# Sliding-window attention and a two-layer tanh-shrink block: another order of the early loads and of the steps of three batches

## The chip, the cores and the metric

The kernel runs on one core of one Trainium2 chip. The metric is the device time of one execution in microseconds. The core has five engines that run side by side and wait for each other through semaphores: TensorE (PE: matrix products; its weight loads are listed apart as PEld), VectorE (DVE), ScalarE (ACT), GpSimd (POOL) and SyncE (SP, which here only issues transfers). Transfers run on 16 DMA engines. ACT and SP issue through hardware queues, GpSimd through a software queue[...].

## The reference, cut to what matters

```python
# q, k, v: [8 batches, 8 heads, 576 positions, 64], float32
scores = scale * np.matmul(q, k.transpose(0, 1, 3, 2))
rel = pos[:, None] - pos[None, :]
mask = (rel >= 0) & (rel < 64)                 # causal window of 64 keys
attn = softmax(np.where(mask, scores, -1e9))
attn_out = np.matmul(attn, v)
x = attn_out.transpose(0, 2, 1, 3).reshape(4608, 512)   # tokens x (heads * dim)
h = x @ w_in                                   # 512 -> 2048, the first layer
g = h - np.tanh(h)
out = g @ w_out                                # 2048 -> 512, the second layer
```

## The kernel before

Two heads make a pair; a batch has four pairs, so pair `g` is pair `g % 4` of batch `g // 4`. A batch has nine blocks of 64 queries; each sees the 64 keys of its own block and the 64 before. The tokens go through the two layers in nine chunks of 512; a chunk has 16 first-layer tiles (`hp_mm`, line L259, then `tanh`, L262, then `g_sub`, L268) and 16 second-layer steps (`yp_mm`, L278). The loop counts half steps `h`: a first-layer tile on each even one, a second-layer step of the chunk before on each odd one from 33 on, and whatever attention work a plan sets beside them:

```python
for h in range(min(items), 2 * (16 * NC + LAG) + 2):      # LAG = 16
    ...
    if h % 2 == 0:
        ...
        if 0 <= c < NC:
            hidden = hp_mm(c, m)
    elif 0 <= cy < NC:
        yp_mm(cy, sy)
    for fn in items.get(h, []):          # the plan's steps
        fn[0](*fn[1:])
    if h % 2 == 0 and 0 <= c < NC:
        g_sub(c, m, *hidden)
```

The first-layer tiles take turns in two PSUM banks (`m % 2`); so tile `m` has to wait for the subtraction of tile `m - 2`.

Batches 0 to 2 (pairs 0 to 11) are placed by a script, `PLAN`; key -1 is what is done ahead of the loop. Each word is a step: a letter, numbers (base 36) and the engines that do it (`p` GpSimd, `a` ACT, `v` DVE, `s` SP). The batches after these follow a fixed pattern that the change leaves alone.

```python
if what in "qr":   load(*n, ...)         # one pair of q, or (r) of k
elif what in "QK": load_all(...)         # a whole batch of q or k, by GpSimd
elif what == "V":  load_v_all(*n)        # a whole batch of v, by GpSimd
elif what == "a":  cast(*n, "q", *eng)   # q of a pair to bf16 rows
elif what == "b":  cast(*n, "k", *eng)
elif what == "v":  load_v(*n)            # one pair of v, by GpSimd
elif what == "d":  cast_v(*n, *eng)      # v of a pair into vb
elif what == "k":  keys_v(*n, *eng)      # "key move": block j, vb -> vw
elif what == "z":  shift_v(...)          # all blocks, upper half of vw -> lower half of the next
elif what == "E":  tr(*n, "q", 3, *eng)  # transposes of q, and two moves to qT
elif what == "F":  tr(*n, "k", ...)      # transposes of k, and a move to kT
elif what == "R":  scores(*n, (4, 0, 1)[n[1]] if n[0] < NP else 4)   # 3 blocks, then exp
elif what == "P":  pv of 9 blocks; norm(*n)
elif what == "X":  x_tr(...)             # transposes of the attention output to xT
# w, o: loads of w_in, w_out; M: masking; i, n, m: constants
```

The parts that V goes through (`vb` and the two `vw` are single buffers, `vb` for all batches, `vw` for even and odd ones):

```python
vw = [const.tile([128, NJ, H, D + 1], BF16, name=f"vw{i}") for i in range(2)]
vb = const.tile([PV, EV, H, D + 1], BF16, name="vb")

def load(g, n, eng):                     # one pair
    if eng is nc.gpsimd:                 # bf16, cast by the transfer, in a part of the batch's tile
        ...
    else:                                # float32, in a tile of its own
        t = qk_pool.tile([P, 2, E * D], F32, tag=n + "f", name=n + "f")
    eng.dma_start(out=t, in_=...)

def keys_v(b, j, eng=nc.sync):           # 64 keys of all heads, 65 KB
    eng.dma_start(out=vw[b % 2][64:128, j]..., in_=vb[8 * j:8 * j + 8]...)

def shift_v(b, j0, j1, eng=nc.sync):
    lo, hi = vw[b % 2][0:64, j0 + 1:j1 + 1], vw[b % 2][64:128, j0:j1]
    if eng is nc.vector:
        eng.tensor_copy(lo, hi)          # on DVE, in two parts
    else:
        eng.dma_start(out=lo..., in_=hi...)

def norm(g):                             # DVE: a reciprocal and two products
    ...
```

Of the kernel before, what the change touches and what calls it, by code (L numbers as in the profile page):

```python
# [15 lines left out]
def kernel(  # L16
# [289 lines left out]
    def play(script):  # L306
        for step in script.split():
# [48 lines left out]

    PLAN = {
        -1: """
            q0a v03 i a0v v00 v02 r0a r1a b0a E0va F0v v01 q1a d02v m q2a d01p R01 r2a q3s
            d00a d03v R02 k00s k07p k01p k02s a1a k03a b1v F1a k04a k05p k08s k06a E1av r3s a2p R12 z0v  # L360
            R00 E2vv R10 K1 n V1 P0 b2a b3p Q1 a3v F2a w0 R11 P1 R22 F3a R21 R20 E3va
            R31 P2 b5p d13a R30 w1 R32 d12v P3 a4p d10a d11a a5a a7p w2 X011v k18s k13s X000v b4p
            k16a k15s k14a k17a X001v X010a b6p k10s k11s k12a Q2 a6p K2 V2 z1s b7p o0 o1 a8p a9p
            o3 b8p d20p F4v d21p d22p d23p E4aa b9p k25s o2 k23p k27s k22s bAp""",
        5: "k26s F5a R41",
        10: "R40 bBp aAp E5av R42 k20s k24s R50 k21s P4",
        11: "R52 E6aa R51 P5 E7vv F6a",
        15: "F7v R60 X100v R62",
        16: "R61 k28s",
        19: "R70 P6 R72 F8a R71 E8av",  # L370
        22: "R80",
        23: "z2s P7",
        24: "E9av",
        26: "X110a aBp X101v",
        27: "R82 F9a R81 X111a",
        30: "FAv M8",
        31: "R92 R91",
        35: "R90 M9",
        41: "P9 FBa EAav",
        43: "P8 RA0 EBaa RA1",  # L380
        45: "RA2 MA",
        50: "X200v PA RB0",
        51: "X201v",
        52: "RB1 RB2",
        53: "MB",
        56: "PB",
        60: "X210v",
        62: "X211a",
    }
# [31 lines left out]
    for h in range(min(items), 2 * (16 * NC + LAG) + 2):  # L421
        n = h // 2
        c, m = divmod(n, M)
# [41 lines left out]
```

The softmax here doesn't subtract the row's maximum and nothing guards it: scores larger than these inputs give would overflow.

## Time and profile before

| | before |
|---|---|
| time, median of 3 | 375.83 us (375.75 to 377.02) |
| span of the profiled execution | 374.0 us |
| busy: PE, DVE, ACT, POOL | 327.9, 213.7, 193.9, 99.6 us |
| first first-layer tile (L259) starts | 44.94 us |
| first second-layer step (L278) in the chain of waits | 90.08 us |
| PE busy from 0 to 75 us, from 75 to 374 us | 39.75 us, 288.19 us |
| moved by DMA | 37.88 MB, mean 101 GB/s |

The profile's page divides the span in 40 slices with the busy share in tenths; the views of the trace (windows, chain of waits, list of waits, timeline) give the same execution in more detail. In all of them `vw<-vb` is a key move, `vw<-vw` the shift, `vall` a load of V, and `ps` the PSUM tile into which every matrix product goes.

### The profile page before, as it was taken

What the parts mean: (1) busy time and instruction counts of PE and PEld (TensorE: products, weight loads), DVE (VectorE), ACT (ScalarE), POOL (GpSimd) and SP (SyncE); (2) the same over time, 40 slices, a digit from 0 to 9 for tenths busy, and PEclk for the clock granted to TensorE, in tenths of its full rate; (3) what the DMA queues carried; (4) which work ended last, traced back from release to release, by engine and by line L of the source; (5) the groups of instructions that cost most, each with busy time, mean ns of one, the idle gap of its engine ahead of it and who ended that gap; (6) DMA issues with size and microseconds to landing.
All of it is one profiled execution on the core that took longest, in us unless ns stands there. A gap on an engine that the chain in (4) does not pass through costs nothing.

```text
span 374.0 us, 6004 instructions
## 1 busy us (share of the span) xinstructions
PE 327.9 (88%) x2289; PEld 192.4 (51%) x2329; DVE 213.7 (57%) x354; ACT 193.9 (52%) x352; POOL 99.6 (27%) x133
## 2 busy tenths in 40 slices
PE   2236565888898999999999999999999999999996
PEld 2226434555554655555555555555555554444442
DVE  2326623686666767777666767676766643443400
ACT  4324454476575665556556556656565344444321
POOL 5606331824417503630543064121000000000000
PEclk9999677699999999999999999999999999999999
DMA  8799998574965855935594458044000001001012
GB/s 180 163 157 152 204 203 160 85 139 78 184 119 96 153 100 129 142 75 106 119 155 80 94 111 142 28 94 112 32 29 30 28 30 56 30 28 56 30 56 84
DMA packets 31980, 37.88 MB, mean 101 GB/s; under 512 B 3536, under 2 KB 25808, under 8 KB 31504
## 3 DMA queue, kind: packets, MB, share of 16 engines
q0 software_dynamic: 19648, 17.45, 31.5%
q1 hardware_dynamic: 10552, 17.82, 16.9%
q10 hardware_dynamic: 1752, 2.24, 2.2%
q8 instruction: 18, 0.29, 0.3%
q14 instruction: 10, 0.08, 0.1%
HBM read 36.70 MB, written 9.44 MB: 123 GB/s over the span
## 4 chain that ended last, share of the span: by engine, by line
PE 78%; DMA 11%; ACT 4%; DVE 3%; issue 2%; ACTq 0%; POOL 0%; DVEq 0%; SPq 0%; POOLq 0%
PE ps L278 33%; PE ps L259 31%; DMA vw<-vb 7%; PE ps L224 4%; PE ps L210 4%; PE ps L197 4%; DMA vw<-vw 2%; PE ps L241 2%; DMA vall<-in_v_dram 2%; DVE xs L235 1%; DVE qt L81 1%; ACT pt L214 1%; ACT th L262 1%; ACT vb L79 1%; ACT kt L79 1%
## 5 line engine op out<-in xcount | busy, mean ns | idle before, releaser
L259 PE MATMUL ps<-xT,wi 128*128 128x512 bf16 x553 | 147.7, 386 | 4.7 <-DVE gT L268 3.1
L268 DVE TENSOR_TENSOR gT<-ps,th 128x512 bf16<-128x512 f32 x144 | 99.2, 690 | 81.4 <-ACT th L262 80.3
L278 PE MATMUL ps<-w_out_sb,gT 128*128 128x512 bf16 x559 | 143.0, 379 | 1.1 <-ACT ysb L283 0.2
L262 ACT ACTIVATE th<-ps 128x512 f32<-128x512 f32 x144 | 86.1, 598 | 83.8 <-PE ps L259 80.0
L259 PEld LDWEIGHTS <-wi 128*128 128x128 bf16 x576 | 61.7, 115 | 50.3 <-issue 7.9
L278 PEld LDWEIGHTS <-gT 128*128 128x128 bf16 x576 | 53.6, 98 | 51.3 <-issue 0.5
L214 ACT ACTIVATE pt<-ps 128x384 bf16<-128x384 f32 x96 | 46.8, 490 | 51.3 <-PE ps L210 37.7
L235 DVE TENSOR_TENSOR xs<-ps,rc 64x576 bf16<-64x576 f32 x64 | 48.3, 755 | 1.5
L210 PE MATMUL ps<-qt,kt 128*128 128x128 bf16 x288 | 37.2, 229 | 10.5 <-DVE qt L81 4.6
L81 POOL COPY vb<-vall 72x1024 bf16<-72x1024 bf16 x25 | 26.2, 1057 | 68.5 <-DMA vw<-vb 45.2
L224 PE MATMUL ps<-vw,pt 128*128 128x130 bf16 x288 | 30.4, 231 | 12.2 <-DVE vw L133 6.2
L224 PEld LDWEIGHTS <-pt 128*128 128x128 bf16 x288 | 23.0, 103 | 25.4 <-issue 8.6
L81 POOL COPY qb<-qall 96x768 bf16<-96x768 bf16 x27 | 22.3, 827 | 48.8 <-PE ps L197 29.1
L81 DVE COPY qt<-ps 64x576 bf16<-64x576 bf16 x31 | 23.5, 758 | 16.8 <-ACT qt L79 15.3
L210 PEld LDWEIGHTS <-kt 128*128 128x128 bf16 x288 | 24.9, 104 | 11.5 <-issue 2.3
L81 POOL COPY kb<-kall 96x768 bf16<-96x768 bf16 x28 | 23.2, 830 | 25.4 <-PE ps L197 9.6
L283 ACT ACTIVATE ysb<-ps 128x512 f32<-128x512 f32 x36 | 21.4, 594 | 15.1 <-PE ps L278 15.1
L79 ACT ACTIVATE qt<-ps 64x576 bf16<-64x576 bf16 x33 | 21.0, 636 | 7.1 <-DMA vw<-vb 3.4
L79 ACT ACTIVATE kt<-ps 128x576 bf16<-128x576 bf16 x28 | 18.1, 646 | 11.7 <-PE ps L197 11.6
L81 DVE COPY xT<-ps 128x512 bf16<-128x512 bf16 (+4 forms) x40 | 13.5, 364 | 16.8 <-PE ps L241 16.8
L197 PE MATMUL ps<-ident,qb 96*128 96x96 bf16 x192 | 15.0, 219 | 5.6 <-DVE qb L81 4.8
L197 PE MATMUL ps<-ident,kb 96*128 96x96 bf16 x192 | 15.2, 221 | 5.1 <-DVE kb L81 3.8
(48 smaller groups left out, 150.4 us busy)
## 6 DMA issues: line engine op xcount, KB each, us to landing
out_dram<-ysb SPq DMA_DIRECT2D x36, 256.0 KB
kall<-in_k_dram POOLq DMA_DIRECT2D x7, 576.0 KB, 9.3
vall<-in_v_dram POOLq DMA_DIRECT2D x7, 576.0 KB, 10.3
qall<-in_q_dram POOLq DMA_DIRECT2D x7, 576.0 KB, 6.2
vw<-vb SPq DMA_DIRECT2D x61, 65.0 KB
vw<-vw SPq DMA_DIRECT2D x7, 520.0 KB
w_out_sb<-in_moe_w_out_dram POOLq DMA_DIRECT2D x4, 512.0 KB, 12.0
wi<-in_moe_w_in_dram POOLq DMA_DIRECT2D x2, 512.0 KB, 9.2
```

Of the source, the lines that this page charges most:

```text
L79: nc.scalar.activation(o, i, ACT.Copy)
L81: eng.tensor_copy(o, i)
L197: nc.tensor.transpose(tp[:, e, :], src[:, e, :], ident[:P, :P])
L210: nc.tensor.matmul(sp[:, i, :], kT[g % NR][:, 64 * j:64 * j + 128], qT[g % NR][:, :, 64 * j:64 * j + 64], start=True, stop=g >= 2 * NP)
L214: nc.scalar.activation(PT[g % NPT][:, 3 * grp:3 * grp + 3, :], sp, ACT.Exp, scale=scale)
L224: nc.tensor.matmul(ps[:, 5 + grp, 130 * i:130 * i + 130], PT[g % NPT][:, j, :], vw[b % 2][:, j, 2 * pr:2 * pr + 2, :], start=True, stop=True)
L235: nc.vector.tensor_tensor(xo[r, :, :, pr, :], ov[r, :, :, h, 0:D], rc[r].to_broadcast([64, 3, 3, 64]), ALU.mult)
L259: nc.tensor.matmul(hp, w_in_tile(ki, m), chunk_tile(c)[:, ki, :], start=(ki == 0), stop=(ki == 3))
L262: nc.scalar.activation(th, hp, ACT.Tanh)
L268: nc.vector.tensor_tensor(gT[c][:, m, :], hp, th, ALU.subtract)
L278: nc.tensor.matmul(yp, gT[c][:, m, s * 128:(s + 1) * 128], w_out_sb[:, m, :], start=(m == 0), stop=(m == M - 1))
L283: nc.scalar.activation(ysb, ps[:, yp_bank(c, s), :], ACT.Copy)
```

## The change

It alters the script only. Among the early loads, four single pairs (k of pairs 1 and 2, q of pairs 2 and 3) now go through GpSimd with the cast on the way, and four (q0, k0, q1, k3) stay in the hardware queues; the loads of V come ahead of most of them. GpSimd does one key move of batch 0 and then issues the whole-batch loads V1 and K1. All nine key moves of batch 1 are issued by SP, and their shift (`z1v`) is done by DVE and no longer by a transfer (`z1s`). Pairs 4 to 11 are set at other half steps: pair 4's value product, `P4`, goes from 10 to 12, pair 5's from 11 to 15, and so on. Its purpose is to let the early loads and key moves of batch 0 through first, to take V of batch 1 off the path, and to spread the attention of three batches over the first-layer tiles in another way.

```diff
     PLAN = {
         -1: """
-            q0a v03 i a0v v00 v02 r0a r1a b0a E0va F0v v01 q1a d02v m q2a d01p R01 r2a q3s
-            d00a d03v R02 k00s k07p k01p k02s a1a k03a b1v F1a k04a k05p k08s k06a E1av r3s a2p R12 z0v
-            R00 E2vv R10 K1 n V1 P0 b2a b3p Q1 a3v F2a w0 R11 P1 R22 F3a R21 R20 E3va
-            R31 P2 b5p d13a R30 w1 R32 d12v P3 a4p d10a d11a a5a a7p w2 X011v k18s k13s X000v b4p
-            k16a k15s k14a k17a X001v X010a b6p k10s k11s k12a Q2 a6p K2 V2 z1s b7p o0 o1 a8p a9p
-            o3 b8p d20p F4v d21p d22p d23p E4aa b9p k25s o2 k23p k27s k22s bAp""",
-        5: "k26s F5a R41",
-        10: "R40 bBp aAp E5av R42 k20s k24s R50 k21s P4",
-        11: "R52 E6aa R51 P5 E7vv F6a",
-        15: "F7v R60 X100v R62",
-        16: "R61 k28s",
-        19: "R70 P6 R72 F8a R71 E8av",
...
+            q0a i v00 a0v v02 v03 v01 d00v d02a r0s b0a r1p q1a E0vv r2p m d03p F0a d01v q3p
+            R01 b2a k05s b1a a1v k00s k08a k01p k02a R02 k04a k06s F1a E1vv q2p V1 a2v R00 R12 K1
+            a3p n k07s F2a Q1 k03s z0v w0 d13p w1 K2 E2aa R11 P0 r3s R10 b3a b5p E3va P1
+            R21 b6p w2 b4p Q2 d10p F3v a4p R20 d11p R22 P2 V2 d12a k17s k12s k16s k10s R30 k18s
+            b7p o3 R32 R31 X001v a7p o2 P3 X010v o0 a5p X000v X011a E4vv a9p b8p""",
+        0: "F4a",
+        10: "R40 k13s F5v k15s E5aa R42 a6v k14s aAp k11s",
+        12: "a8p d20p R41 d23p d21p d22p z1v k24s E6av F6a k27s R50 k25s b9p o1 P4",
+        15: "R51 R52 R61 F7a k22s P5 R62 bAp R60 E7va",
+        16: "k21p",
+        19: "bBp P6 X100a R71 k20s k28s F8a k23s k26s R70",
+        20: "R72 E8vv",
+        23: "X101a z2s R80 E9aa P7 R81",
...
```

The rest of the script, half steps 22 to 56, goes over in the same manner: the same steps at other places.

## The prediction

> **What bounds the kernel now.** I read the page's slices first, then the windows by stage, then the chain of waits, then the list of waits, and last the timeline of the first 75 us.
>
> The slices (9.35 us each) show two kernels in one span:
>
> ```profile
> PE   2236565888898999999999999999999999999996
> PEclk9999677699999999999999999999999999999999
> DMA  8799998574965855935594458044000001001012
> ```
>
> From the tenth slice on TensorE is full. In the first eight it is not, and there the DMA row is full and the clock row dips. The windows put numbers on it (columns: busy time of PE, PEld, DVE, ACT, POOL with instruction counts, then granted clock, DMA share, GB/s):
>
> ```profile
> 20.00:25.00 5.00, 1.30 (x11) 0.88 (x9) 0.64 (x1) 1.22 (x2) 0.00 (x0) 1.00 1.15 201
> 40.00:45.00 5.00, 3.16 (x30) 2.84 (x31) 2.93 (x8) 1.87 (x3) 0.00 (x0) 0.55 1.13 197
> 60.00:65.00 5.00, 2.46 (x26) 2.15 (x24) 1.23 (x3) 1.13 (x3) 0.06 (x1) 0.60 0.71 130
> 80.00:90.00 10.00, 8.00 (x77) 5.36 (x77) 7.82 (x14) 7.37 (x16) 0.77 (x1) 1.00 0.75 130
> 150.00:200.00 50.00, 49.63 (x376) 29.39 (x381) 35.27 (x58) 30.19 (x57) 20.43 (x26) 1.00 0.62 111
> ```
>
> The windows up to 75 us add up to 39.8 us of PE busy time. The page has 327.9 us in all, so the 299 us after that hold 288.1 us, 96%. The change leaves the number of TensorE instructions as it is. So nothing can be won after 75 us; what can be won is idle or half-speed TensorE time before, 35 us idle in all. What keeps TensorE waiting there is told by the chain (start, length, what):
>
> ```profile
> 3.48 6.24 DMA vall<-in_v_dram
> ...
> 14.26 12.39 DMA vw<-vb
> ...
> 40.58 6.71 DMA vw<-vb
> 47.30 5.79 DMA vw<-vb
> ...
> 53.24 9.35 DMA vw<-vw
> 62.63 1.05 PE ps L224 x8
> ```
>
> This is one dependency told twice. V of batch 0 comes in, is packed into vb, and nine "key moves" carry it to vw; the last lands at 26.64. Only then may vb be overwritten with batch 1; its key moves run from 40.58 to 53.09, and a tenth transfer shifts them down within vw (520 KB, 9.35 us). The value product of pair 4 (L224) waits for it until 62.63. After that TensorE does not stop again. The list of waits says who stood still (total, times, longest):
>
> ```profile
> DVE gT L268 <- ACT th L262: 80.3, 90, 4.4
> ...
> POOL vb L81 <- DMA vw<-vb: 45.2, 3, 15.6
> ...
> ACT qt L79 <- DMA vw<-vb: 3.4, 1, 3.4
> ...
> PE ps L224 <- DMA vw<-vw: 2.4, 1, 2.4
> ```
>
> The first line is the biggest and means nothing: it is spread over 90 tiles while PE is full. The ACT line is the interesting one. ACT issued four of batch 1's key moves; the last had to wait in ACT's queue until 47.30, when an earlier move was complete. That held back the first tanh to 49.28, and PE stood 2.6 us (48.07 to 50.66) before its third first-layer tile.
>
> **What the Trainium skill says.** "DMA: Bandwidth & Descriptors", section "Issuing engines are not separate DMA queues": transfers started by ScalarE, SyncE or GpSimd end on the same 16 engines and interleave. The trace agrees: DMA share is 1.15 in 20 to 25 us while one 65 KB key move is under way for 12.39 us; the same kind of move took 4.3 to 5.3 us where landing is given. So where a bulk load is issued matters only through its time. "TensorE: Matmul & The Clock Gate", section "Part 1: The HAM clock gate": TensorE runs at half rate until it has been busy for about 3.4 us, and falls back after an idle window. The timeline agrees: 128-column matmuls start 0.107 us apart up to 33.8 us and 0.056 us after, and 512-column ones 0.43 us apart at 45 to 51 and 62 to 71 us, 0.215 us later.
>
> **The change, part by part.**
>
> (1) *Packing V of batch 0.* Before, vb is complete at 12.20 us (last DVE copy 11.84 + 0.36). After, V is first in the GpSimd queue with q0 and k0 alone beside it, so about 0.3 to 0.5 MB less has to move before V; at the 212 GB/s of the window 5 to 10 us that is some 1.5 us. But the last copy on DVE stands behind two q moves (1.5 us) and the constants (0.54 + 0.09 + 1.04 us). From 7.0 us, my estimate for the first V: 0.43 + 1.5 + 1.7 + 0.43 = 11.1 us. Gain about 1 us.
>
> (2) *Key moves of batch 0.* Five on SyncE, three on ACT, one on GpSimd. ACT's come late: its order is V copy, k cast, k move, exp, two casts (1.07 + 0.84 + 0.65 + 0.49 + 2 x 0.84 us and waits between), so its first is issued at about 14 us and its last at 16.5, as late as before (16.1). V1 and K1 are issued at about 13.4 and 14.2, earlier than before (17.43 and 15.37), but q2, k2 and q3 no longer sit in the same hardware queues ahead of the moves. I take 24.5 us for the last landing, against 26.64: gain 2 us, and this is my softest number.
>
> (3) *From there to the first first-layer tile.* Before: 26.64 to 44.94, 18.3 us. After, the same four pairs: shift by DVE 1.4, then value products that alternate with normalisations (1.75 us each), scores and two moves between, and transposes of x at the end. Worked through I get 18.5: no gain. First layer starts at about 43 us.
>
> (4) *From there to pair 4's value product.* Before 44.94 to 62.63, 17.7 us. Three things go. All nine key moves of batch 1 are on SyncE, which has nothing else to do, so ACT's stall goes: 2.6 us of PE. The shift is two DVE copies of 0.70 us in place of 9.35 us. Pair 4 comes two half steps later, behind seven first-layer tiles and eight other pieces. Is V in time? GpSimd's order after 24.5: copy 1.04, two issues 1.6, two casts 1.7, issue 0.8, cast 0.84, issue 0.8, copy 1.04, cast 0.83, copy 1.04: 36 us with waits; nine issues at 0.71 us and landings of about 6 us: 49 us; shift: 51 us. TensorE is there later: six tiles from 43 us, one per 1.4 us (two buffers; 0.86 or 1.72 + 0.60 + 0.69 for each turn), are 51.5; then scores in one buffer, each of which waits for an exp of 0.49 us, four sets of transposes and one more tile, some 5.3 us. Pair 4 at 57. So V is no longer the limit, TensorE's own order is. Gain 5.6 us.
>
> (5) *To full TensorE.* Before, seventh tile at 68.72, 6.1 us after pair 4. After, 6 us on, TensorE stands at about 63 us, and it has then done more: tiles seven and eight (2 x 0.86 us) and pair 6's scores (3 x 0.34 us) and a set of transposes, 3.1 us that needn't be done later.
>
> Sum: 68.7 - 63 + 3.1 = 8.8 us. Of the time of 375.8 us that leaves 367.0. The rest of the list, pairs 6 to 11 in a new order, I count as zero; I take off half a microsecond for a clock that is up sooner. Predicted 366.5 us.
>
> **The rivals.**
>
> *A: the bulk loads are in the way.* V1, K1 and Q1 are issued before ACT's key moves are. If the last move then lands at 27 to 29 us, steps 3 to 5 all shift by that. For it: before, that move landed just as DMA went quiet (0.50 share in 25 to 30 us), that is, when all was drained. Against: nothing else is queued in the hardware queues now. Time 369 to 372.
>
> *B: TensorE stays at half rate.* The stretch of 43 to 63 us holds some 14 us of full-rate TensorE work. If it never warms up there, this is 28 us and TensorE itself is the limit: 5 to 7 us lost, time 372 to 374. Against: before, the clock came up at 53.3 us after 8 us of such work, with a stall in it.
>
> *C: the order of pairs 4 to 11 makes new waits.* DVE is 7.82 of 10 us busy at 80 to 90 us and ACT 7.37; a bad order gives back 2 to 4 us. Or, the other way, pair 4's work spread over more tiles fills the gaps in that stretch (PE 8.00 of 10) and brings 2 us more.
>
> *D: key moves land early,* at 21 us, as fair shares would have it: another 3.5 us, time 363.
>
> **Range and chances.** 360 to 373.5 us: from D with C's good side to A or B alone. 2% is 7.5 us, so faster by over 2% means below 368.3. My sum is 1.8 us beyond that, with an uncertainty of some 5 us: 0.58. Within 2%: 0.34. Slower by over 2% needs A, B and C at once, or a stall I don't see: 0.08.
>
> **What would show it.** In the profile of the changed kernel: no 520 KB transfer vw<-vw in the chain before 70 us; no ACT wait on vw<-vb; last key move of batch 0 between 23 and 26 us; first L259 at 42 to 44; pair 4's L224 at 55 to 59 with its last release from an exp or from PE, not from a DMA or L133; PE full from about 63 us. Wrong if L133 of batch 1 waits long on vw<-vb and holds the gT subtractions behind it, if the first L259 is later than 45 us, or if PE in 80 to 120 us is less busy than before.

## The result and the profile after

The kernel after takes 363.62 us (median; 363.34 to 365.53), the kernel before beside it 375.79 us. The ratio is 0.9681, with a 95% interval of 0.9641 to 0.972: 12 us, 3.2%, less. The span of the profiled execution went from 374.0 to 362.1 us.

The slices of the page, in the order in which they were shown of before (PE, granted clock, DMA; a slice is 9.05 us now):

```profile
PE   0538667889999999999999999999999999999995
PEclk9999998999999999999999999999999999999999
DMA  8899992377876567655935592250000010010012
```

TensorE starts later (the first slice is 0 and was 2), and from the second slice on it is as full as before or fuller. Of the dip in the clock row (6, 7, 7, 6 in slices five to eight) one 8 is left. Up to 34 us the clock reads 1.00 in both kernels although products of 128 columns start 0.107 us apart there, twice the 0.056 us of later; in that stretch the spacing of the products shows the rate, and the clock column does not. The same windows as before (busy time of PE, PEld, DVE, ACT, POOL, then clock, DMA share, GB/s):

```profile
20.00:25.00 5.00, 1.41 (x13) 1.25 (x14) 0.20 (x1) 1.78 (x3) 0.00 (x0) 1.00 1.21 241
...
40.00:45.00 5.00, 4.35 (x28) 2.22 (x27) 3.54 (x5) 3.01 (x7) 3.49 (x6) 1.00 1.21 222
...
60.00:65.00 5.00, 4.42 (x57) 3.44 (x55) 2.86 (x5) 3.57 (x8) 2.64 (x3) 1.00 0.02 3
...
80.00:90.00 10.00, 9.30 (x72) 5.31 (x70) 6.08 (x10) 6.36 (x13) 5.59 (x6) 1.00 0.61 99
```

The wait at 20 to 25 us is still there: TensorE 1.41 us busy, DMA at 241 GB/s. From 40 us on it is another picture: 4.35 us in place of 3.16, at full clock, and 4.42 in place of 2.46 at 60 to 65 us, where DMA has run dry (3 GB/s, was 130). In all, 45.4 us of TensorE time lie in the first 75 us (39.75 before). The chain of waits (start, length, what):

```profile
13.62 15.74 DMA kall<-in_k_dram
...
36.15 6.37 DMA vw<-vb
42.53 6.29 DMA vw<-vb
...
53.41 1.32 DVE vw L133
...
54.77 0.59 PE ps L224 x4
```

The 520 KB transfer of 9.35 us is gone; its place has a DVE copy (L133). But the key moves of batch 1 still stand on the chain ahead of pair 4's product (L224), which goes on 7.9 us sooner than before (54.77, was 62.63). K of batch 1, 15.74 us under way, is on the chain where batch 0's key moves were. The list of waits:

```profile
POOL vb L81 <- DMA vw<-vb: 53.9, 4, 15.4
...
PE ps L224 <- DVE vw L133: 7.1, 3, 4.2
...
DVE vw L133 <- DMA vw<-vb: 5.0, 1, 5.0
```

No line has ACT waiting for vw<-vb any more. The last line is the shift of batch 0; ahead of the one of batch 1 DVE stood 2.88 us, which the view puts down to no one. TensorE waits for L133 instead of the transfer: 4.2 us once in batch 0 (25.91), and 1.97 + 0.85 us in batch 1, as its timeline has it:

```profile
51.34 0.22 PE L224 MATMUL ps<-vw,pt 128*128 128x130 bf16 x1
53.53 0.39 PE L224 MATMUL ps<-vw,pt 128*128 128x130 bf16 x4 [1.97 <-DVE vw L133]
54.77 0.59 PE L224 MATMUL ps<-vw,pt 128*128 128x130 bf16 x4 [0.85 <-DVE vw L133]
```

Set side by side, the stages were shortened by these amounts (times of the two traces):

| event | before | after | gained so far |
|---|---|---|---|
| vb of batch 0 complete | 12.20 | 10.81 | 1.4 |
| its last key move landed | 26.64 | 25.16 | 1.5 |
| first first-layer tile | 44.94 | 40.1 | 4.8 |
| pair 4's product, last wait over | 62.63 | 54.77 | 7.9 |
| first second-layer step | 89.9 | 77.5 | 12.4 |
| third result tile (L283) | 118.06 | 105.61 | 12.4 |
| end of the span | 374.0 | 362.1 | 11.9 |

So all of it is gained by the first second-layer step (PE's timeline of before, then of after):

```profile
89.92 1.03 PE L278 MATMUL ps<-w_out_sb,gT 128*128 128x512 bf16 x4
77.49 1.03 PE L278 MATMUL ps<-w_out_sb,gT 128*128 128x512 bf16 x4
```

Up to there each trace has 459 matmuls, so the work behind that point is as good as the same. TensorE was busy with it for 52.09 us of 89.92 before and for 47.68 us of 77.49 after. Of the 12.4 us, then, some 8.0 are less standing still and 4.4 are the same products done faster. That is less time at half rate, an estimate from these two sums: before, the products from 41.3 to 53.3 and from 62.6 to 71 us run at half rate, after only those from 54.8 to 57.4, besides the stretch up to 34 us in both. How much of the second part only follows from the shorter waits no run sets apart.

### The profile page after: what moved, and what is told of

Read it like the earlier page. It is cut to its first block, busy times and chain, and to the rows that moved or that the text cites. A ratio compares the mean times of both kernels' runs of the same rounds, so it can differ in the third digit from the quotient of the medians.

```text
span 362.1 us, 6043 instructions
## 1 busy us (share of the span) xinstructions
PE 326.2 (90%) x2329; PEld 189.5 (52%) x2329; DVE 214.7 (59%) x352; ACT 192.8 (53%) x355; POOL 103.6 (29%) x136
## 4 chain that ended last, share of the span: by engine, by line
PE 73%; DMA 15%; issue 5%; POOL 3%; ACT 2%; DVE 2%; SPq 0%; POOLq 0%; ACTq 0%; DVEq 0%
PE ps L278 32%; PE ps L259 29%; DMA vw<-vb 7%; DMA kall<-in_k_dram 4%; PE ps L224 4%; PE ps L197 3%; PE ps L210 3%; DMA vall<-in_v_dram 2%; PE ps L241 2%; DMA vw<-vw 1%; POOL kb L81 1%; POOL vb L81 1%; DVE qt L81 1%; ACT th L262 1%; POOL qb L81 0%
## 5 line engine op out<-in xcount | busy, mean ns | idle before, releaser
L259 PE MATMUL ps<-xT,wi 128*128 128x512 bf16 x576 | 148.2, 381 | 1.0 <-DVE gT L268 0.9
L278 PE MATMUL ps<-w_out_sb,gT 128*128 128x512 bf16 x576 | 145.2, 379 | 0.2 <-ACT ysb L283 0.2
L259 PEld LDWEIGHTS <-wi 128*128 128x128 bf16 x576 | 61.3, 114 | 47.0 <-issue 2.7
L81 POOL COPY vb<-vall 72x1024 bf16<-72x1024 bf16 x28 | 29.4, 1060 | 71.3 <-DMA vw<-vb 53.9
L224 PE MATMUL ps<-vw,pt 128*128 128x130 bf16 x288 | 30.6, 229 | 8.5 <-DVE vw L133 7.1
L224 PEld LDWEIGHTS <-pt 128*128 128x128 bf16 x288 | 22.7, 102 | 22.5 <-issue 7.6
L81 DVE COPY qt<-ps 64x576 bf16<-64x576 bf16 x33 | 25.0, 757 | 12.9 <-ACT qt L79 8.3
L81 POOL COPY kb<-kall 96x768 bf16<-96x768 bf16 x28 | 23.6, 847 | 28.9 <-DMA kall<-in_k_dram 11.1
L283 ACT ACTIVATE ysb<-ps 128x512 f32<-128x512 f32 x36 | 21.4, 594 | 15.1 <-PE ps L278 15.1
L81 DVE COPY xT<-ps 128x512 bf16<-128x512 bf16 (+4 forms) x35 | 12.1, 368 | 16.8 <-PE ps L241 16.8
L79 ACT ACTIVATE qt<-ps 64x576 bf16<-64x576 bf16 x31 | 19.7, 635 | 3.5 <-PE ps L197 1.9
L79 ACT ACTIVATE kt<-ps 128x576 bf16<-128x576 bf16 x30 | 19.4, 645 | 2.6 <-PE ps L197 1.5
L197 PE MATMUL ps<-ident,kb 96*128 96x96 bf16 x192 | 14.4, 214 | 5.7 <-ACT kb L79 4.6
```

Of the source, the lines that this page charges most:

```text
L79: nc.scalar.activation(o, i, ACT.Copy)
L81: eng.tensor_copy(o, i)
L197: nc.tensor.transpose(tp[:, e, :], src[:, e, :], ident[:P, :P])
L224: nc.tensor.matmul(ps[:, 5 + grp, 130 * i:130 * i + 130], PT[g % NPT][:, j, :], vw[b % 2][:, j, 2 * pr:2 * pr + 2, :], start=True, stop=True)
L259: nc.tensor.matmul(hp, w_in_tile(ki, m), chunk_tile(c)[:, ki, :], start=(ki == 0), stop=(ki == 3))
L278: nc.tensor.matmul(yp, gT[c][:, m, s * 128:(s + 1) * 128], w_out_sb[:, m, :], start=(m == 0), stop=(m == M - 1))
```

## The experiments

Three parts of the change could be set apart: the **early part** (loads, order up to the first tile, all key moves of batch 1 on SP), the **loop order** (at which half steps pairs 4 to 11 come) and the **shift** of batch 1 (DVE or transfer). Theory M, the prediction's, has most of the gain in the path of V of batch 1, after the first first-layer tile; E has it in the early part; D has it in the backlog of transfers, which lets V of batch 1 land only when everything queued has drained. (This D is not rival D of the prediction.)

### The shift alone

```diff
-... K2 V2 z1s b7p o0 ...            # kernel before
+... K2 V2 b7p o0 ...
-10: "... k21s P4"
+10: "... k21s z1v P4"
```

> Kernel before, but the shift of batch 1 in vw by two DVE copies just ahead of pair 4's value product, in place of the 520 KB transfer. Theory M (the prediction's: most of the gain is the path of V of batch 1, after the first first-layer tile): the last key move lands at 53.1 as before, TensorE reaches pair 4 at 59.9 and no longer waits there to 62.6, so 2.5 us less: 373.3. Theory E (most of the gain is the early part, up to the first tile): the wait of 2.5 us is soaked up by waits that follow, 375 to 376. Theory D (DMA backlog governs: V of batch 1 lands when everything queued has drained): one transfer of 520 KB less, 373 to 374, and the key moves of batch 2 land earlier too.

Measured: ratio 0.990 (0.9877 to 0.9923), 3.8 us less. Pair 4 waits for no transfer; L133 stands at 58.45 with both copies in 1.31 us. That is more than the 2.5 us of M and the 2 to 3 of D, which this run doesn't tell apart, and E, with 0 to 1, fell.

### The key moves of batch 1 on SP alone

```diff
-k16a k15s k14a k17a ... k10s k11s k12a     # kernel before
+k16s k15s k14s k17s ... k10s k11s k12s
```

> Kernel before, but all nine key moves of batch 1 issued by SP (four of them were ACT's). M: ACT's stall of 3.4 us goes, the first tanh starts at about 46 instead of 49.3 us, first-layer tiles 3 to 6 come 2.6 us sooner; but pair 4 still waits for the shift by transfer to about 62 us, so alone it brings 0 to 1 us: 375 to 375.8. E: 0. D: 0, the nine moves wait in the same backlog; landing of the last at 53 us again.

Measured: 1.0039 (1.0014 to 1.0063), 1.5 us slower. ACT's stall is gone, and yet the end is later. The chain of this run says why:

```profile
41.23 6.26 DMA vw<-vb
47.50 8.20 DMA vw<-vb
...
55.85 8.47 DMA vw<-vw
```

The ninth move starts when the first has landed (47.50, as on ACT before), but lands at 55.7 and not at 53.1, and pair 4 goes on at 64.37 (62.63 before). In this trace the moves also start 0.65 us later and the first tile 1.2 us later than before; products are at half rate until about 39 us here (33.8 before). The stall of TensorE that was saved, 2.6 us, lies ahead of that wait and is lost in it. That SP has nothing else to do does not make the moves land sooner.

### The loop order alone, and the early part alone

```diff
 # early_before: all steps ahead of the loop as before; in the loop the places of after
 # early_after: steps up to the first tile as after; then, still ahead of the loop,
+ F4v k13s k15s k14s k11s a6p a8p z1s d20p d21p d22p d23p b9p o1 k25s k23p k27s k22s bAp
 # and in the loop the places of before
```

> Early part of the kernel before (all steps ahead of the loop, with its ACT-issued key moves of batch 1 and its shift by transfer), steps in the loop at the places of the kernel after. M: pair 4 comes behind seven tiles, so TensorE has work while V is under way, but ACT's stall stays and V is there at 62.6: 369 to 371, about half of the gain. E: the loop's order alone brings little, 374 to 376. D: as M, since V lands as late as before: 370 to 372.

> Early part of the kernel after (its loads, its order up to the first tile, all key moves of batch 1 on SP), then the rest of the early steps of before with the shift by transfer, and the loop's steps at the places of before. M: first tile at 40 to 41 us, ACT's stall gone, but pair 4 at the shift's end (key moves landed at 52, shift 6 to 9 us: 59 to 61) : 371 to 373. E: first tile 4.8 us sooner and most of the 12.2 us with it, 365 to 367. D: landing of the key moves at 52 as in the kernel after, shift on top: 371 to 372.

Measured: loop order alone 0.9938 (0.9911 to 0.9964), 2.3 us; early part alone 0.9953 (0.9931 to 0.9976), 1.8 us. For the loop order M had 5 to 7 us, D 4 to 6 and E 0 to 2; for the early part M had 3 to 5, D 4 to 5 and E 9 to 11. So none of the three is right about both. In early_after the first tile comes at 42.2 us, but the list of waits has

```profile
PE ps L224 <- DMA vw<-vw: 7.5, 1, 7.5
```

What was won ahead of pair 4 is lost in this wait (2.4 us before): it goes on at 60.5 us.

### Two of the three parts

```diff
 # a_shift_dma: kernel after
-12: "a8p d20p R41 d23p d21p d22p z1v k24s ..."
+12: "a8p d20p R41 d23p d21p d22p z1s k24s ..."
 # ea_shift_dve: early_after without z1s, and
-10: "... k21s P4"
+10: "... k21s z1v P4"
 # eb_shift_dve: early_before without z1s, and
-12: "R41 k24s E6av F6a R50 P4"
+12: "R41 k24s E6av F6a R50 z1v P4"
```

> Kernel after with the shift of batch 1 done by one transfer again (z1s in place of z1v). If the DVE shift is what lets the other two parts count: last key move lands at 52.4, the transfer takes 8 to 9 us, pair 4 goes on at 61 us, seven tiles done by then: 368 to 370, so 5 to 6 us slower than after. If the parts simply add up (shift alone 3.8, loop order alone 2.3, early part alone 1.8 us): 367.4.

> Early part of after, the loop's places of before, shift of batch 1 by DVE. If the parts add up: 375.9 - 3.8 - 1.8 = 370.3. If the early part's gain was only hidden behind the shift by transfer (in early_after TensorE waited 7.5 us for it): key moves land at 52 us, pair 4 at 54 us in place of 60.5, 366 to 367.

> Early part of before, the loop's places of after, shift of batch 1 by DVE. If the parts add up: 375.9 - 3.8 - 2.3 = 369.8. If shift and loop order help each other (behind seven tiles, pair 4 finds V just there): 366 to 368. ACT's stall on its fourth key move stays here, 2.6 us of TensorE.

> Once more: early part of before, the loop's places of after, shift of batch 1 by DVE. The first time most executions lay some 9 us above the fastest (368.1), so no ratio. If parts add up 369.8; if shift and loop order help each other 366 to 368.

Measured, with the single parts again (us: one less the ratio, times 375.8):

| early part | loop order | shift by DVE | ratio | interval | us less |
|---|---|---|---|---|---|
| | | x | 0.990 | 0.9877 to 0.9923 | 3.8 |
| | x | | 0.9938 | 0.9911 to 0.9964 | 2.3 |
| x | | | 0.9953 | 0.9931 to 0.9976 | 1.8 |
| x | x | | 0.9916 | 0.9892 to 0.9941 | 3.2 |
| x | | x | 0.9807 | 0.9752 to 0.9862 | 7.3 |
| | x | x | 0.9762 | 0.9716 to 0.9808 | 8.9 |
| x | x | x | 0.9681 | 0.9641 to 0.972 | 12.0 |

The shift is the largest part in every row: 3.8 us alone, 5.5 on top of the early part, 6.6 on top of the loop order, 8.8 on top of both. Each number is good to 1 to 2 us, so that for pairs of parts the surplus over the sum is within the noise or near it; for all three it is not (7.9 as a sum, 12.0 together). The reason is seen best for the early part: with the transfer in place it mostly lengthens TensorE's wait for it, from 2.4 us to 7.5 in early_after and 6.46 in a_shift_dma, where pair 4 goes on at 61.22. The loop order alone leaves that wait as it was (2.1 us); its 2.3 us come from elsewhere. a_shift_dma, expected at 368 to 370, came out at 371.7, and ea_shift_dve at 368.1, between its two readings.

The row of loop order and shift has to be read with care. Executions of this kernel spread from 363.44 to 378.18 us, with a median of 375.69 in 20, as long as the kernel before beside it (375.05), and the ratio counts only the four nearest to the fastest. The 8.9 us are what this combination can bring, and the 6.6 with them, not what it brings as a rule. The two profiled executions, of 376.85 and 377.53 us, look alike at the shift. From the second, first DVE's shift, then GpSimd's copies of the same stretch (start, length, engine, line):

```profile
60.38 6.54 DVE L133 COPY vw<-vw 64x2080 bf16<-64x2080 bf16 x2
```

```profile
60.18 0.84 POOL L81 COPY kb<-kall 96x768 bf16<-96x768 bf16 x1
60.95 4.03 POOL L81 COPY vb<-vall 72x1024 bf16<-72x1024 bf16 x4
64.92 0.82 POOL L81 COPY kb<-kall 96x768 bf16<-96x768 bf16 x1
```

Two DVE copies that took 1.31 us in the first experiment take 6.54 us. In the chain of waits the first has 5.93 us of it, and ends 0.6 us after GpSimd's row of six copies. The Trainium skill, "SBUF — State Buffer", section "SBUF: two separate sides", calls the port pair that DVE and GpSimd share an exclusive lock: of a GpSimd operation and a DVE operation in a two-port mode (or with two inputs in SBUF), the one that starts first holds it for the whole instruction and the other is blocked. In which mode these copies run no trace shows, but the times fit. This trace also has something that the sentence does not say: a whole row of six GpSimd copies kept one DVE copy out. In the kernel after it was not so. There GpSimd's copies of V of batch 2, which stand ahead of the shift in the script as well, ran at 63.13 us, and in the stretch of the shift were three short copies, with which DVE took turns:

```profile
52.31 2.41 DVE L133 COPY vw<-vw 64x2080 bf16<-64x2080 bf16 x2 [2.88 <-issue]
```

```profile
52.88 1.29 POOL L81 COPY kb<-kall 96x768 bf16<-96x768 bf16 x1
54.12 1.29 POOL L81 COPY qb<-qall 96x768 bf16<-96x768 bf16 x1
```

What decides between the two is open, and so is how much of the spread of 14.7 us comes from it; the shift itself lost 5.2 us.

### The clock

```diff
+def filler(n):      # products that nobody reads
+    for i in range(n):
+        nc.tensor.matmul(ps[:, 6, 400:512], ident, ident[:, 0:112], start=True, stop=True)
-... E2aa R11 P0 r3s ...
+... E2aa R11 tk tk P0 r3s ...        # tk: 20 fillers
-12: "... b9p o1 P4"
+12: "... b9p o1 tk tk P4"
```

> Kernel after with 40 idle products of 112 columns (identity on identity, into columns of PSUM that nobody reads) ahead of pair 0's value product and 40 more ahead of pair 4's, where TensorE stands waiting: they only keep its clock up. Theory E (the early gain is clock): the steps from 26 to 34 us run at full rate, first first-layer tile at 37.5 in place of 40.2 us, and the end comes 2 us sooner: 361.5. Theory M: the first tile comes sooner too, but pair 4 still waits for V until 54 us; only the half-rate stretch of 55 to 57 us goes, 1 us: 362.5 to 363.5.

> The kernel after itself on the same chip as the other runs of this group, for comparison: 363.6, key moves of batch 1 landed at 52.3, pair 4 resumed at 53.5 to 54.8.

Measured: 362.38 us with the fillers, 362.35 us (ratio 0.967, 0.9637 to 0.9704) for the kernel after on the same chip. No gain. The windows of the run with fillers:

```profile
20.00:25.00 5.00, 4.67 (x50) 4.51 (x48) 0.00 (x0) 1.78 (x3) 0.00 (x0) 1.00 1.23 244
25.00:30.00 5.00, 1.61 (x22) 1.37 (x22) 4.09 (x6) 1.22 (x2) 4.30 (x5) 0.83 1.25 197
30.00:35.00 5.00, 5.00 (x49) 4.72 (x48) 3.51 (x7) 3.08 (x5) 3.96 (x6) 0.50 1.27 205
```

Ahead of pair 0 the fillers do fill the wait, and the clock comes up (pair 0's products take 0.39 us in fours, at 26.1). But then TensorE has work for 1.61 us of 5, the clock falls, and at 30 to 35 us it is at half. The longest gap in that stretch is 1.43 us, so the prediction's "falls back after an idle window" has to be read as a window with little work in it. First tile at 41.0 us, as without the fillers. Ahead of pair 4 they did what they should: the tile behind it took 1.03 us, where it took 1.91 in the kernel after. That was worth nothing at the end either; after_2 had full rate there (1.03 us) without them. So the 37.5 us that E foretold for the first tile were not put to the test, as the stretch from 29.8 to 35 us stayed at half rate. What a_warm and after_2 do show is that the clock of the first tiles made no difference to the end here: after_2 has the first one at half rate (1.91 us for its four products) and a_warm at full (1.03), both start at 41.0, and both kernels end alike.

### The key moves on ACT again

```diff
-... P2 V2 d12a k17s k12s k16s k10s R30 k18s     # kernel after
+... P2 V2 d12a k17a k12a k16a k10s R30 k18s
-10: "... a6v k14s aAp k11s"
+10: "... a6v k14a aAp k11s"
```

> Kernel after with four of the nine key moves of batch 1 issued by ACT again (12, 16, 17 and 14). M: ACT waits in its queue for earlier moves, tanh comes late, TensorE loses 2 to 3 us around 42 to 48 us; but pair 4 waits for V anyway: 364 to 366. If it is the issue on one queue that makes V late (the ninth move waits for the first to land), two queues bring the last landing forward from 52 to about 48 us, and pair 4 to 51.5: 361 to 362.

Measured: 0.9872 (0.9828 to 0.9916); 369.61 us, 7.3 us slower than the kernel after beside it. ACT's timeline:

```profile
32.39 1.06 ACT L79 ACTIVATE vb<-vall 72x1024 bf16<-72x1024 bf16 x1
35.31 1.90 ACTq L127 DMA_DIRECT2D vw<-vb  x3
37.26 1.26 ACT L214 ACTIVATE pt<-ps 128x384 bf16<-128x384 f32 x3 [3.81 <-issue]
...
53.36 0.61 ACTq L127 DMA_DIRECT2D vw<-vb  x1
```

ACT reaches the three issues at 33.45 us, but V is packed at 35.3 by GpSimd, and all that while pair 3's exps stand behind them: 3.81 us. Pair 3's product waits 3.63 us for them, and the first tile comes at 43.7 (41.0 in after_2). The fourth move stands behind six tanh and is issued at 53.36, whereas SP had issued all nine by 43.1 in the kernel after; pair 4 goes on at 60.3. So both hold in this run: the issues stalled ACT, and the last went out late. M had the direction and at most a third of the size. The other reading, V sooner by two queues, did not come; with one issue ten us late, the run doesn't say what two queues with nothing else to do would bring.

### The backlog of bulk loads

```diff
-... o3 ... o2 ... o0 ...      12: "... b9p o1 P4"      16: "k21p"
+                              12: "... b9p P4"         16: "k21p o0 o1 o2 o3"
```

> Kernel after with the four loads of the second layer's weights (4 MB read) moved behind the key moves of batch 1, to half step 16. If the DMA backlog decides when these key moves land (DMA is full from 30 to 55 us): last landing at 46 to 48 in place of 52.4 us, pair 4 at 51.3 when TensorE gets there, TensorE stays at full rate, 359 to 361. If the moves are bound by their own issue and by the queue slots they wait for: no change, 363.6. The weights are needed at about 80 us; issued at 62, they land at 76.

Measured: 0.9848 (0.9792 to 0.9903), 369.08 us, slower than the kernel after by some 5.5 us (6.3 by the ratios). Pair 4's product went on at 53.03 and 54.27, half a microsecond sooner than in the kernel after, though DMA moved 166 GB/s in 30 to 55 us in place of 213. So the weights' loads hardly delayed the key moves of batch 1, and D, as far as these four loads go, fell. The relief came late, however: from 30 to 45 us DMA moved 211 GB/s in both, and only after that less, when all nine moves had been issued. Moved, they met the key moves and the shift of batch 2 and the weights' own first use (PE's timeline):

```profile
79.35 1.02 PE L278 MATMUL ps<-w_out_sb,gT 128*128 128x512 bf16 x4 [1.00 <-DMA w_out_sb<-in_moe_w_out_dram]
...
86.45 1.02 PE L278 MATMUL ps<-w_out_sb,gT 128*128 128x512 bf16 x4 [1.48 <-DMA w_out_sb<-in_moe_w_out_dram]
91.69 0.63 PE L224 MATMUL ps<-vw,pt 128*128 128x130 bf16 x8 [2.43 <-DMA vw<-vw]
```

## Why the prediction was right, and where it was not

366.5 us was foretold, with 360 to 373.5; it is 363.6. The working summed to 8.8 us; there were 12. Step by step:

(1) and (2), V of batch 0: 11.1 and 24.5 us foretold, 10.81 and 25.16 found. The mechanism was right; the second gain is 1.5 us and not 2. Rivals A and D of the prediction (27 to 29, and 21 us) did not come.

(3), from there to the first tile, **is the term that was mis-sized most**: "I get 18.5: no gain". It took 14.9 us against 18.3 before, so 3.4 us that were not foretold, while the whole sum fell short by 3.2. Between pair 1's and pair 2's products lie 3.5 us (5.4 before: there pair 2 stood behind q moves of ACT, PE idle for 1.52 us at 35.92). That stretch runs wholly at half rate in the kernel after and only up to 33.8 us in the kernel before, so its 1.9 us are the order of the steps and not the clock. From pair 3's products to the first tile lie 4.7 us (6.1 before). Here order and clock both changed: five of x's 18 transposes are now ahead of pair 3, and the rest run at full rate, 0.66 us for nine where before it was 1.14 and 1.12 us. The two were not set apart, and which piece of the 18.5 us was too long the prediction does not show.

(4), from the first tile to pair 4: 3.6 us foretold for this stretch alone (17.7 to 14.1), 3.1 found (14.6). The size was right and **the mechanism was half wrong**, so that the size is in part luck. "So V is no longer the limit, TensorE's own order is": TensorE reached pair 4 at 51.34 us, not at 57, since six tiles took 1.17 us each and not 1.4 and what followed them was quicker too; V's shift was complete at 54.73 and not at 51, since the last move landed at about 52.3 and DVE's copies took 2.41 us and not 1.4. So pair 4 still waited for V. And of the three causes named, the moves' going to SP brings nothing by itself (1.5 us lost in b_keys_sp), though in the kernel after it is needed (7.3 us lost with four of them on ACT); the shift by DVE is the one that counts, 8.8 us on top of the other parts.

(5), to full TensorE: 3.2 us foretold. From pair 4 to the first second-layer step 4.6 us were found (27.3 to 22.7); the rest, counted as zero, gave half a microsecond back. "After that TensorE does not stop again" was not quite so in the kernel before: it stood up to 1.01 us at a time (83.98 us) in the stretch of rival C, whose good side this may be. But before, half rate went on to about 71 us after pair 4 and now ends at 57.4, and for a clock that is up sooner the prediction had taken off half a microsecond. Order and clock are not set apart here either.

Rival B, half rate, did not come: TensorE was at full rate from 34.2 to 54.8 us. Three of the signs named were wrong: the first L259 was to be at 42 to 44 (40.1), pair 4's last release from PE or an exp (it was L133), and PE full from about 63 us (3.94 of 5 us at 65 to 70). A sign of being wrong came in part: the seventh tile's tanh was done at 50.4 us, and its gT stood behind the shift until 57.35. TensorE's waits for gT come to 0.9 us in all, so that cost it little.

What stays open is why the key moves of batch 1 take until about 52.3 us. Taking the weights' four loads out of the way from 45 us on brought half a microsecond; the other loads beside the moves weren't moved.

## What to carry to other kernels

Follow a buffer's whole round (load, pack, move, shift, use, overwrite) and take out the longest link first; until then, what is won ahead of it is waited out at that link (7.5 us in early_after), and parts of a change measured one by one look worth less than they are together (7.9 us and 12.0). In these runs a transfer that waits for data was better issued by an engine that has nothing else in its queue (7.3 us), but that alone did not make it land sooner. When a bulk load is put off, look at what it will meet there.

## What the runs showed of the hardware

A DVE copy of 64 x 2080 bf16 within SBUF, 0.70 us alone, took 5.93 us beside a row of six GpSimd copies. In the kernel after, DVE's two copies took 2.41 us together, and GpSimd's copies of 96 x 768 beside them 1.29 us each in place of 0.83. The same shift as one transfer of 520 KB took 9.35 us before. The last of batch 1's nine key moves was issued just when the first had landed, whether one engine issued them all (42.53 in the kernel after) or two did (47.30 before). A TensorE clock that 3.94 us of fillers had brought up fell again although TensorE was not idle for longer than 1.43 us at a time, only busy for 1.61 us in 5.
